# Lower parts of the first three weight blocks by TensorE and ScalarE, and the copy of an expert step's result moved behind the splits

## The chip, the cores and the metric

The kernel runs on one core of a Trainium2 chip. The metric is the device time of one execution in microseconds (us). A core has five engines that work beside each other, each through its own list of instructions in order: TensorE (PE in the profile; its weight loads are PEld), VectorE (DVE), ScalarE (ACT), GpSimd (POOL) and SyncE (SP), which here only starts transfers (DMA). An instruction that needs another engine's result waits for a semaphore, and everything behind it on its engine waits too.

## What is computed

Three layers in a row on 2 sequences of 768 tokens with 384 channels. First, a linear attention with 8 heads whose state decays by `w` per token. Second, a layer norm and a dense layer of width 1536 with a ReLU. Third, a mixture of 8 experts, where each token goes to one expert (or to that of the token before it, by a gate).

```python
def _attn_ref(r, k, v, w, u):
    for t in range(S):
        cur = np.einsum('bhd,bhe->bhde', u[None] * kt, vt)
        y[:, :, t] = np.einsum('bhd,bhde->bhe', rt, state + cur)
        state = w[None, :, :, None] * state + np.einsum('bhd,bhe->bhde', kt, vt)
def _moe_ref(x, g_ln, w_ch1, w_ch2):
    xn = (x - mu) / np.sqrt(var + 1e-06) * g_ln
    return x + np.maximum(xn @ w_ch1, 0.0) @ w_ch2
def _moe2_ref(x, w_gate, w_local, w1, w2):
    ...
            h = np.maximum(x[b, s] @ w1[e], 0.0)
            out[b, s] = p[e] * (h @ w2[e])
```

## The kernel before, in words

Products that need full precision are made of two numbers of the fast f32 form each: a high part (the value rounded by a copy into that type) and a low part (the value minus the high part). A product is then three fast matmuls: high by high, high by low, low by high.

**The first stretch, a list written out by hand.** Everything up to the experts is a list of small tasks in one string, `ORDER`; each word is a call (`w_lo:p.1` is the function `w_lo` on POOL for block 1), and each engine gets its instructions in the order of the words. The attention goes by pairs of (sequence b, group g of 128 tokens); the dense layer's weights come in 12 blocks f of 128 x 768. One block passes these tasks: `ld_c` (transfer of packed words), `dec0`, `dec1`, `dec2` on DVE (they unpack the words into one of two buffers, `d_[f % 2]`), `w_g` on ACT (three multiplications by the norm's gain), `w_hi` on ACT (high part into `wh`), `w_lo` on DVE or POOL (low part into `wl`). `dec0` of block f+2 overwrites the buffer that block f's last reader has used. Before the change `w_lo` runs on POOL for blocks 0 and 1 (`w_lo:p.0`, `w_lo:p.1`) and on DVE for block 2.

For a group of tokens the attention's tasks are: `kt`, `L`, `knt`, `rka`, `rkb` (products on DVE or POOL), `c` (sums; eight ACT instructions with their reads), `cv`, `at` (PE, 16 small matmuls), `am` (mask, DVE), `u` (PE), `us` (ACT copies it into the state `R`), `uw` (decay, by ACT, DVE or POOL), `ss`, `y` (PE), `yx` (DVE adds), `yq` (ACT squares), `yr`, `ym`, `ln` (norm, POOL or DVE), `lt` (PE turns the rows), `lh` and `ll` (high part on ACT, low part on DVE). Then the dense layer runs: `m1` (18 matmuls), `hh` (ACT), `hl` (DVE), `m2` per sequence. The first `m1` stands behind `lt.0.0` and `u.0.1` on PE.

**The experts.** For each expert e and each tile t of 128 of its tokens, `step(e, t)` is written out; steps with t > 0 stand in a branch that is taken when the expert has that many tokens. An engine that doesn't take the branch goes through a short piece of code that waits for its open transfers and then raises the semaphores by what the branch would have raised them. In this run the steps are (0,0), (1,0), (2,0), (2,1), (2,2), (3,0), (4,0), (4,1), (4,2), (5,0), (5,1), (6,0), (6,1), (7,0). The matmuls of a step: `first_pe` (first layer, banks 0 and 1; half of it for t = 0 at the step's head), `turn_pe` (turns the hidden layer of the step before), `xpose_pe` (turns gathered rows), `second` (second layer of the step before, into bank 4). On ACT and DVE: `xpose_split` and `turn_split` (high part on ACT, low part on DVE), `first_act` (ReLU), and for t = 0 `fl` (high and low parts of the coming weights). `result(o)` copies bank 4 into an output buffer on ACT and starts, on POOL, an indirect transfer that scatters it; `get` starts, on POOL, the indirect gather of a coming tile's rows into `x`, `xp` or `xe`. `rows(2,2)` is fetched by a `get` in step (2,0).

The order inside a step with t > 0 on ACT is: the copy of `result`, the high part of `xpose_split`, two high parts of `turn_split`, two `first_act`. For t = 0: the copy, one `fl`, two high parts of `turn_split`, `first_act`, two `fl`, `first_act`, `xpose_split`, three `fl`.

Of the kernel before, what the change touches and what calls it, by code (L numbers as in the profile page):

```python
# [49 lines left out]
y.1.0 w_g.2 ld_T.1.1 y.0.0 w_lo:p.1 ld_c.3 L:d.1.1.0 kt:p.1.1 yx.1.0 yq.1.0 ld_c.4 w_hi.2 cv:p.0.0.0 dec0.3 dec1.3 L:p.1.1.1  # L50
cv:p.0.0.1 yx.0.0 yq.0.0 yr.1.0 at.1.1 ym:d.1.0 ym:p.0.0 ln:p.1.0 lt.1.0 yr.0.0 ln:p.0.0 ld_k.0.1 knt:p.0.1 dec2.3 ld_v.0.1
w_lo:d.2 dec0.4 ss.0.0 dec1.4 dec2.4 w_g.3 w_hi.3 ld_v.1.1 lt.0.0 ld_k.1.1 lh.0.0 lh.1.0 w_g.4 w_hi.4 ll.0.0 w_lo:p.3 ld_T.0.1
ll.1.0 L:p.0.1.1 u.0.1 m1.0 ld_c.5 kt:p.0.1 L:p.0.1.0 dec0.5 dec1.5 dec2.5 w_g.5 w_lo:d.4 rka:d.1.1 sw:p.0.0 ld_c.6 dec0.6
rka:p.0.1 hh.0 rkb:p.0.1 dec1.6 w_hi.5 ld_c.7 hl.0 us.0.1 m1.1 hh.1 w_lo:p.5 dec2.6 hl.1 m2.0.0 m2.1.0 knt:p.1.1 dec0.7 dec1.7
m2.0.1 dec2.7 uw:p.0.1 ss.0.1 w_g.6 ld_c.8 w_hi.6 w_lo:p.6 am.1.1 ld_c.9 dec0.8 m2.1.1 dec1.8 c:a.0.1 rkb:p.1.1 w_g.7 at.0.1
am.0.1 w_hi.7 c:a.1.1 ld_c.10 m1.2 dec2.8 ld_k.1.2 w_g.8 hh.2 ld_k.0.2 w_lo:p.7 u.1.1 sw:p.1.0 m1.3 us.1.1 cv:p.1.1.0 cv:p.0.1.0
hh.3 w_hi.8 cv:p.1.1.1 dec0.9 dec1.9 hl.2 y.1.1 yx.1.1 dec2.9 yq.1.1 ym:a.1.1 y.0.1 cv:p.0.1.1 yx.0.1 yq.0.1 uw:p.1.1 consts
m2.1.2 hl.3 m2.0.2 w_g.9 w_hi.9 ym:d.0.1 m2.1.3 yr.1.1 ln:p.1.1 ss.1.1 lt.1.1 w_lo:d.8 yr.0.1 ln:d.0.1 dec0.10 ld_T.0.2 ld_c.11
lt.0.1 lh.0.1 m2.0.3 kt:p.0.2 w_lo:d.9 m1.5 sw:d.1.1 lh.1.1 ll.0.1 ll.1.1 m1.4 dec1.10 dec2.10 ld_T.1.2 kt:p.1.2 hh.5 L:p.1.2.1
hl.5 m2.1.5 m2.0.5 hh.4 dec0.11 w_g.10 w_hi.10 dec1.11 hl.4 m2.1.4 dec2.11 ld_v.0.2 w_g.11 rka:p.0.2 w_hi.11 rkb:p.0.2 m2.0.4  # L60
L:p.0.2.1 c:d.0.2 m1.7 hh.7 ld_v.1.2 rka:p.1.2 rkb:d.1.2 w_lo:d.11 w_lo:p.10 m1.6 sw:d.0.1 hl.7 hh.6 hl.6 c:d.1.2 m2.0.7
# [4 lines left out]
knt:d.1.3 yx.1.2 hh.11 rd.1.0 rl.0 hl.11 yr.0.2 knt:d.0.3 rm:d.0 m2.0.10 yq.1.2 yr.1.2 ln:p.0.2 rn.0 lt.0.2 rc.0 arg.0 ym:a.1.2
ln:p.1.2 lt.1.2 rkb:p.1.3 lh.0.2 lh.1.2 ll.0.2 m2.0.11 ll.1.2 ex.0 cv:p.0.3.0 L:p.0.3.1 x2.0.1 L:p.1.3.1 m2.1.11 x2.1.1 ld_v.0.4
row.0 m1.12 rr.0 hh.12 scan.0 col.0 L:d.1.3.0 oh.0 m1.13 hh.13 sum.0 hl.12 m2.1.12 rank.0 m1.14 pos.0 m2.0.12 c:d.1.3 hh.14
cv:p.0.3.1 hl.13 hl.14 m2.1.13 m2.0.13 ld_v.1.4 ld_k.1.4 m2.1.14 m2.0.14 sw:p.1.2 at.0.3 am.0.3 ld_T.0.4 cv:p.1.3.1 m1.15 hh.15
u.0.3 val.0 rw.0 tab.0 add.0 ld_k.0.4 m1.16 sw:a.0.2 us.0.3 hl.15 at.1.3 rka:p.0.4 m2.1.15 rt.0.1 uw:d.0.3 ss.0.3 y.0.3  # L70
rkb:p.0.4 c:a.0.4 ld_v.0.5 am.1.3 u.1.3 knt:p.1.4 yx.0.3 xs.0.1 us.1.3 uw:d.1.3 hh.16 yq.0.3 cv:p.0.4.1 re.0.1 ss.1.3 m1.17
xs.1.1 rt.1.1 y.1.3 hl.16 rd.0.1 re.1.1 ym:a.0.3 rd.1.1 m2.1.16 cv:p.1.3.0 yx.1.3 yq.1.3 hh.17 rka:d.0.5 hl.17 rl.1 m2.0.15
rm:a.1 rn.1 yr.0.3 sw:a.0.3 m2.0.16 ln:p.0.3 lt.0.3 rc.1 ym:p.1.3 arg.1 L:d.0.4.0 yr.1.3 ln:p.1.3 ld_T.1.4 L:p.1.4.1 lt.1.3
L:d.1.4.0 row.1 lh.0.3 lh.1.3 ll.0.3 rr.1 scan.1 ll.1.3 m2.1.17 x2.1.2 xs.1.2 m2.0.17 x2.0.2 rka:p.1.4 col.1 oh.1 m1.18 hh.18
# [4 lines left out]
uw:d.1.4 ss.1.4 y.1.4 hl.22 hl.23 L:p.0.5.0 yx.0.4 yq.0.4 arg.2 ex.2 yx.1.4 yr.0.4 ym:d.0.4 L:d.0.5.1 ln:d.0.4 yq.1.4 ym:a.1.4
m2.0.22 row.2 rr.2 scan.2 m2.0.23 xs.0.2 x2.0.3 m2.1.22 lt.0.4 yr.1.4 ln:d.1.4 lt.1.4 lh.0.4 rkb:d.1.5 sum.2 lh.1.4 sw:p.1.4  # L80
m2.1.23 cv:p.0.5.1 ld_T.1.5 rt.0.3 col.2 ll.0.4 at.0.5 knt:p.1.5 x2.1.3 ll.1.4 m1.24 L:p.1.5.0 am.0.5 hh.24 hl.24 oh.2 m1.25
knt:p.0.5 re.0.3 m2.1.24 xs.1.3 rt.1.3 xs.0.3 rank.2 m1.26 u.0.5 cv:d.0.5.0 rd.0.3 hh.25 hl.25 val.2 re.1.3 L:p.1.5.1 rd.1.3
# [1079 lines left out]
```

## Time and profile before

| | us |
|---|---|
| median of 3 runs | 461.54 (458.67 to 463.55) |
| the profiled execution | 460.63 |
| its span (first to last instruction) | 458.8 |
| PE busy | 390.6 (85%) |
| DVE busy | 310.3 (68%) |
| POOL busy | 203.9 (44%) |
| ACT busy | 187.7 (41%) |

Times in views count from the span's start. A row of the timeline has start, duration, engine, line, operation and `out<-in`; `[2.67 <-ACT xq L141]` says that the engine sat idle for 2.67 us before it and what ended that. `x3` is a run of three instructions merged into one row, whose duration reaches from the first to the last one's end. A busy engine isn't at its peak: matmuls overlap, so the step from one start to the next tells more of them than their durations. A name followed by q (ACTq, POOLq) is that engine's sequencer.

### The profile page before, as it was taken

To read this page: it belongs to the slowest core of one execution; us is meant where nothing else is said; L and a number is where in the kernel's file an instruction comes from. 1 tells how busy PE (TensorE), PEld (TensorE's weight loads), DVE (VectorE), ACT (ScalarE), POOL (GpSimd) and SP (SyncE) were. 2 spreads that over 40 slices of the span, in tenths; PEclk is the share of its full clock that TensorE was granted. 3 is DMA by queue.
4 is the path that set the end of the run, shared out by engine and by line. 5 is a ranking of instruction groups with operands and counts; after the bars stand their busy time and mean duration, and the time that the engine had idled before them with its cause. 6 is when DMAs were issued, how large, how long until landed. Compare 5 with 4: busy or idle time off the path is not lost. (4 is left out here: it accounts for less than half of the span.)

```text
span 458.8 us, 8752 instructions
## 1 busy us (share of the span) xinstructions
PE 390.6 (85%) x3297; PEld 356.0 (78%) x3297; DVE 310.3 (68%) x605; ACT 187.7 (41%) x447; POOL 203.9 (44%) x231
## 2 busy tenths in 40 slices
PE   1435496799979988999999999889889999999993
PEld 1434495799969978998999998777778788898883
DVE  7998999965873688478764877977711782265440
ACT  1365265331411441312131625448623872566450
POOL 5878978736361191128130020072453663423321
PEclk9999889899989999999999999999989999999997
...
GB/s 237 312 168 259 69 194 219 0 23 209 33 5 113 25 96 17 179 4 34 3 4 306 3 94 391 135 242 261 298 307 42 57 310 297 40 150 19 10 24 16
DMA packets 25360, 59.70 MB, mean 130 GB/s; under 512 B 4506, under 2 KB 11110, under 8 KB 25024
## 3 DMA queue, kind: packets, MB, share of 16 engines
...
HBM read 57.92 MB, written 5.70 MB: 139 GB/s over the span
## 5 line engine op out<-in xcount | busy, mean ns | idle before, releaser
L514 PE MATMUL banks<-wh,H 128*128 128x384 f32 x288 | 83.9, 353 | 8.1 <-DVE H L502 6.5
L981 PE MATMUL banks<-w1h,xq 128*128 128x512 f32 x168 | 59.3, 414 | 7.5 <-ACT xq L141 2.7
L514 PEld LDWEIGHTS banks<-wh,H 128*128 128x128 f32 x288 | 53.7, 193 | 10.3 <-DVE H L502 7.5
L146 DVE TENSOR_TENSOR w2l<-wb,w2h 128x1024 fp32r<-128x1024 f32 (+1 forms) x33 | 33.1, 1027 | 41.6 <-ACT w2h L141 41.3
L499 ACT ACTIVATE H<-banks 128x512 fp32r<-128x512 f32 x36 | 21.3, 594 | 78.5 <-PE banks L495 73.3
L514 PE MATMUL banks<-wl,H 128*128 128x384 f32 x144 | 49.3, 343 | 0.0
L1004 PE MATMUL banks<-w2h,H 128*128 128x384 f32 x224 | 46.4, 340 | 0.3 <-ACT H L141 0.3
L981 PEld LDWEIGHTS banks<-w1h,xq 128*128 128x128 f32 x168 | 32.2, 192 | 17.6 <-ACT xq L141 3.7
L495 PE MATMUL banks<-xq,wh 128*128 128x256 f32 x216 | 44.7, 305 | 0.4 <-DVE xq L478 0.4
L1004 PEld LDWEIGHTS banks<-w2h,H 128*128 128x128 f32 x224 | 39.2, 188 | 1.2 <-ACT H L141 0.5
L495 PEld LDWEIGHTS banks<-xq,wh 128*128 128x128 f32 x216 | 36.8, 207 | 1.1 <-DVE xq L478 0.6
L502 DVE SCALAR_TENSOR_TENSOR H<-banks,H 128x512 fp32r<-128x512 f32 x36 | 24.4, 684 | 17.7 <-ACT H L499 17.5
L202 POOL DMA_INDIRECT x<-xd,ids x17 | 20.0, 1179 | 34.4 <-issue 16.3
L981 PE MATMUL banks<-w1l,xq 128*128 128x512 f32 x84 | 34.1, 406 | 0.2 <-DVEq L1069 0.2
L146 DVE TENSOR_TENSOR w1l<-wa,w1h 128x512 fp32r<-128x512 f32 (+1 forms) x36 | 32.5, 952 | 0.4 <-ACT w1h L141 0.2
L495 PE MATMUL banks<-xq,wl 128*128 128x256 f32 x108 | 32.1, 297 | 0.0
L495 PE MATMUL banks<-xuh,wh 128*128 128x256 f32 x108 | 31.3, 290 | 0.0
L495 PE MATMUL banks<-xul,wh 128*128 128x256 f32 x108 | 30.6, 284 | 0.5 <-DVE xul L478 0.5
L495 PE MATMUL banks<-xuh,wl 128*128 128x256 f32 x108 | 30.5, 283 | 0.0
L141 ACT ACTIVATE w2h<-wb 128x1024 fp32r<-128x1024 f32 (+1 forms) x33 | 28.4, 900 | 3.1 <-DMA wb<-in_w 3.1
L372 POOL TENSOR_TENSOR cv<-R,c 64x384 f32<-64x384 f32 x19 | 18.7, 990 | 24.4 <-DVE c L367 22.7
L141 ACT ACTIVATE w1h<-wa 128x512 fp32r<-128x512 f32 (+1 forms) x36 | 28.1, 852 | 0.0
...
## 6 DMA issues: line engine op xcount, KB each, us to landing
...
```

What stands on the lines that cost most here:

```text
L141: ACT.activation(out=dst_hi, in_=src, func=ACTF.Relu if relu else ACTF.Copy)
L146: (lo_eng or DVE).tensor_tensor(out=dst_lo, in0=src, in1=dst_hi.bitcast(F32), op=ALU.subtract)
L202: POOL.indirect_dma_start(dst, None, xd[0:n, :], IndirectOffsetOnAxis(ap=off, axis=0), bounds_check=n - 1, oob_is_err=False)
L372: e.tensor_tensor(out=r3(cv[b][s], NH), in0=r3(R[b][g % 2][s, q, :], NH), in1=bc(c[s], [64, NH, HD]), op=ALU.mult)
L495: PE.matmul(out=ph[:, i, :], lhsT=a, rhs=x_[:, k, :], start=(q == 0), stop=(q == 8))
L499: ACT.activation(out=hh[:, ring(n)], in_=r3(B[3 + n % 2], 2), func=ACTF.Relu)
L502: DVE.scalar_tensor_tensor(out=hl[:, ring(n)], in0=r3(B[3 + n % 2], 2), scalar=0.0, in1=hh[:, ring(n)].bitcast(F32), op0=ALU.max, op1=ALU. ...
L514: PE.matmul(out=bank_o(b, g), lhsT=a[:, f2, s][:, i], rhs=w_[:, 2 * p + i, DM:], start=(p + i + n == 0), stop=(p == NP - 1 and i == 1 and ...
L981: PE.matmul(out=B[n], lhsT=a_[:, k, t], rhs=w_[:, k, n * 512:n * 512 + 512], start=(last == 0 and q == 0), stop=(last == 1 and q == KD - 1))
L1004: PE.matmul(out=B[4][:, 0:DM], lhsT=a_[:, k, 0:128], rhs=w_[:, k, :], start=(q == 0), stop=(q == 23))
```

## The change

Two parts. First, the lower parts of blocks 0, 1 and 2 are made by PE and ACT: `lo_pe` puts ident x block minus ident x high part into banks 3 and 4 (for each half a matmul of plain f32 and one of the fast form with the negated identity, which `negid` writes once into an unused corner of `H`), and `lo_act` copies both banks into `wl`. `w_lo` of these three blocks leaves POOL and DVE. Second, `result(o)` in `step` moves from behind `turn_pe` to behind `turn_split`.

```diff
 ORDER = """
...
+rka:d.1.0 at.0.0 rkb:p.1.0 w_g.0 w_hi.0 wlp.0 am.1.0 u.1.0 dec0.1 dec1.1 dec2.1 c:a.1.0 wla.0 w_g.1 cv:d.1.0.1 ld_k.0.0
+knt:p.0.0 w_hi.1 wlp.1 us.1.0 am.0.0 ld_v.0.0 u.0.0 rka:p.0.0 rkb:d.0.0 c:a.0.0 us.0.0 uw:a.0.0 wla.1 cv:p.1.0.0 ld_c.2 dec0.2
...
+        neg = H[:, 1, KE - 1, 0:128]
+
+        def negid():
+            ACT.activation(out=neg, in_=ident, func=ACTF.Copy, scale=-1.0)
+
+        def lo_pe(f):
+            for i in range(2):
+                c = slice(i * DM, i * DM + DM)
+                PE.matmul(out=B[3 + i][:, 0:DM], lhsT=ident, rhs=d_[f % 2][:, c].bitcast(F32), start=True, stop=False)
+                PE.matmul(out=B[3 + i][:, 0:DM], lhsT=neg, rhs=wh[:, f, c], start=False, stop=True)
+
+        def lo_act(f):
+            ACT.activation(out=wl[:, f].rearrange("p (i d) -> p i d", i=2), in_=BB[:, 3:5, 0:DM], func=ACTF.Copy)
...
             if before is not None:
                 for n in range(2):
                     turn_pe(n)
-                result(o)
             if t:
                 xpose_split(1)
                 first_pe(e, 1, 0, 1)
...
             if before is not None:
                 for n in range(2):
                     turn_split(n)
+                result(o)
             first_act(e, t, 0)
```

In the list, `wlp` is `lo_pe` and `wla` is `lo_act`. The order of DVE, POOL and SP changes only by the three `w_lo` that go. On PE, between the second group's first products and the next attention product, before the change (d_116 and d_117 are the two block buffers, R, L and knt those of the attention, 111 and 131 of sequence 1, 109 and 130 of sequence 0):

```order
L405 MATMUL banks<-R_111,knt_131 48x48 x16
L405 MATMUL banks<-R_109,knt_130 48x48 x16
L441 MATMUL banks<-R_111,L_125 64x48 x16
L441 MATMUL banks<-R_109,L_124 64x48 x16
L388 MATMUL banks<-L_125,kt_123 64x64 x16
```

The same place on PE after the change, from the second half of `lo_pe` of block 1 on (lines are 15 higher in the changed file):

```order
L309 MATMUL banks<-d_117,cs 128x384
L310 MATMUL banks<-wh,H 128x384
L420 MATMUL banks<-R_109,knt_130 48x48 x16
L456 MATMUL banks<-R_111,L_125 64x48 x16
L456 MATMUL banks<-R_109,L_124 64x48 x16
L309 MATMUL banks<-d_116,cs 128x384
L310 MATMUL banks<-wh,H 128x384
L309 MATMUL banks<-d_116,cs 128x384
L310 MATMUL banks<-wh,H 128x384
L403 MATMUL banks<-L_125,kt_123 64x64 x16
```

`lo_pe` of block 1 now stands ahead of `u.0.0`, and that of block 2 ahead of `at.1.1`, behind which `lt.1.0` and `lt.0.0` follow.

On ACT, from `us.0.0` on, before the change:

```order
L412 ACTIVATE R_109<-banks 48x384
L421 ACTIVATE ws_134<-R_109,wC 48x48 x8
L292 ACTIVATE d_116<-d_116,gt_s 128x128 x3
L456 ACTIVATE xh_75,sq_143<-x_72,sx_139 128x384
L295 ACTIVATE wh<-d_116 128x768
L456 ACTIVATE xh_74,sq_142<-x_72,sx_138 128x384
```

The same place on ACT after the change:

```order
L427 ACTIVATE R_109<-banks 48x384
L436 ACTIVATE ws_134<-R_109,wC 48x48 x8
L313 ACTIVATE wl<-banks 128x768
L292 ACTIVATE d_116<-d_116,gt_s 128x128 x3
L471 ACTIVATE xh_75,sq_143<-x_72,sx_139 128x384
L295 ACTIVATE wh<-d_116 128x768
L471 ACTIVATE xh_74,sq_142<-x_72,sx_138 128x384
L313 ACTIVATE wl<-banks 128x768
```

`lo_act` of block 1 stands between `uw:a.0.0` and `w_g.2`, ahead of `yq.1.0`; that of block 2 behind `yq.0.0`.

On ACT in the experts, step (2,0) and the head of step (2,1), before the change (x_147, xh_74 are output buffers, w1h and w2h high parts of weights, H the turned hidden layer):

```order
L1010 ACTIVATE xh_74<-banks 128x384
L141 ACTIVATE w2h_2944<-wb_2535 128x1024
L141 ACTIVATE H<-banks 128x4x128 x2
L986 ACTIVATE hs<-banks,tab 128x512
L141 ACTIVATE w2h_2944<-wb_2535 128x1024 x2
L986 ACTIVATE hs<-banks,tab 128x512
L141 ACTIVATE xq<-banks 128x3x128
L141 ACTIVATE w1h_2536<-wa_2946 128x1024 x3
L762 TENSOR_LOAD nt_i
L1069 COMPARE_AND_BRANCH
L1010 ACTIVATE x_147<-banks 128x384
L141 ACTIVATE xq<-banks 128x3x128
```

The same place after the change, from the splits of the turned layer on:

```order
L141 ACTIVATE H<-banks 128x4x128 x2
L1025 ACTIVATE xh_74<-banks 128x384
L1001 ACTIVATE hs<-banks,tab 128x512
L141 ACTIVATE w2h_2957<-wb_2548 128x1024 x2
L1001 ACTIVATE hs<-banks,tab 128x512
L141 ACTIVATE xq<-banks 128x3x128
L141 ACTIVATE w1h_2549<-wa_2959 128x1024 x3
L777 TENSOR_LOAD nt_i
L1084 COMPARE_AND_BRANCH
L141 ACTIVATE xq<-banks 128x3x128
L141 ACTIVATE H<-banks 128x4x128 x2
L1025 ACTIVATE x_147<-banks 128x384
```

The copy (L1010, now L1025) stands behind the two splits into H, in a step with t = 0 as in one with t > 0; `xq` of a step with t > 0 is now its first ACT instruction.

## Rows read from the trace of the kernel before

**Rows 1.** Busy time by stretch: us, PE, PEld, DVE, ACT, POOL, PEclk, DMA.

```profile
20.00:45.00 25.00, 11.44 (x168) 9.82 (x169) 22.79 (x28) 13.92 (x48) 20.20 (x18) 1.00 0.65 219
...
110.00:330.00 220.00, 205.56 (x1990) 189.79 (x1989) 160.37 (x424) 81.83 (x203) 71.10 (x84) 0.99 0.33 117
```

**Rows 2.** Waits of PE over the whole span: us in total, times, longest.

```profile
PE banks L514 <- DVE H L502: 6.5, 2, 5.0
...
PE banks L981 <- ACTq L1069: 2.3, 3, 0.9
...
PE banks L208 <- DMA x<-xd,ids: 1.2, 1, 1.2
```

**Rows 3.** Timeline of the first 64 us, single rows of four engines.

```profile
10.42 1.97 PE L388 MATMUL banks<-L,kt 48*64 48x64 f32 x32
...
17.43 1.81 POOL L298 TENSOR_TENSOR wl<-d,wh 128x768 fp32r<-128x768 f32 x1
...
17.75 1.90 DVE L277 TENSOR_SCALAR d<-wq 128x768 int32<-128x768 int32 x1
...
20.56 1.52 PE L405 MATMUL banks<-R,knt 64*48 64x48 f32 x32 [1.62 <-POOL knt L353]
...
24.04 0.84 ACT L295 ACTIVATE wh<-d 128x768 fp32r<-128x768 f32 x1
...
29.04 0.46 ACT L412 ACTIVATE R<-banks 48x384 f32<-48x384 f32 x1
...
29.54 1.91 ACT L421 ACTIVATE ws<-R,wC 48x48 f32<-48x48 f32 x8
...
31.46 0.99 ACT L292 ACTIVATE d<-d,gt_s 128x128 f32<-128x128 f32 x3
...
34.54 0.56 DVE L277 TENSOR_SCALAR d<-wq 128x768 int32<-128x768 int32 x1
...
34.65 0.61 ACT L456 ACTIVATE xh<-x,sx 128x384 f32<-128x384 f32 x1 [2.20 <-DVE x L445]
...
41.48 0.90 PE L469 MATMUL banks<-cs,xh 128*128 128x128 f32 x3 [1.62 <-POOL xh L464]
...
42.94 1.02 DVE L478 TENSOR_TENSOR xq<-banks,xq 128x384 fp32r<-128x384 f32 x2 [0.71 <-ACT xq L473]
...
44.89 1.68 DVE L277 TENSOR_SCALAR d<-wq 128x768 int32<-128x768 int32 x1 [0.93 <-POOL wl L298]
...
60.39 0.52 PE L514 MATMUL banks<-wl,H 128*128 128x384 f32 x1
...
60.71 0.84 PE L514 MATMUL banks<-wh,H 128*128 128x384 f32 x2
```

**Rows 4.** Timeline of steps (2,1) and (2,2), single rows of three engines.

```profile
330.65 0.49 PE L208 MATMUL banks<-cs,x 128*128 128x128 f32 x3
...
333.76 0.49 ACT L1010 ACTIVATE x<-banks 128x384 f32<-128x384 f32 x1 [3.75 <-DMA out<-first_o,oi]
...
334.69 0.79 PE L981 MATMUL banks<-w1h,xq 128*128 128x512 f32 x1 [2.67 <-ACT xq L141]
...
335.85 1.00 POOL L202 DMA_INDIRECT x<-xd,ids  x1 [0.31 <-ACT H L141]
...
344.66 0.49 PE L208 MATMUL banks<-cs,x 128*128 128x128 f32 x3
...
345.79 0.50 PE L981 MATMUL banks<-w1h,xq 128*128 128x512 f32 x1
```

**Rows 5.** Busy time by stretch about that gap, columns as in rows 1.

```profile
332.00:334.60 2.60, 0.01 (x1) 0.00 (x0) 0.00 (x0) 0.84 (x3) 0.11 (x1) 1.00 0.59 198
334.60:338.00 3.40, 3.31 (x8) 2.64 (x9) 1.78 (x3) 1.01 (x3) 2.79 (x3) 0.50 0.88 276
```

**Rows 6.** Instructions of the branch's line on POOL, 326 to 335 us.

```profile
L1069 POOLq INC_SWDGE_SEM  x1: 485/485/485, 333.1 to 333.1; - x1
```

**Rows 7.** Gathers that POOL issued between 335.5 and 337 us.

```profile
DMA to landing us min/median/max: 7.9/8.0/8.1
```

More of the change, by code (lines that the diff above doesn't have):

```diff
@@ L50 @@
[L50 to L61, printed above, removed]
@@ L66 @@
[L66 to L74, printed above, removed]
@@ L79 @@
[L79 to L82, printed above, removed]
@@ L91 @@
-lw.1 x2.1.5 rt.0.5 re.0.5 ext.0 exh.0 rd.0.5 rt.1.5 xs.1.5 exl.0 re.1.5 rd.1.5 ext.1 exh.1 exl.1 rl.5 rm:d.5 e1.1 f0.2 f0.10
-zX.0 rn.5 rc.5 arg.5 e1.0 row.5 f0.7 f0.1 f0.9 f0.8 f0.11 ex.5 sum.5 e1.2 e1h.1 e1l.1 rr.5 scan.5 col.5 e1h.0 e1l.0 oh.5 val.5
-rank.5 pos.5 e1h.2 e1l.2 e1.3 e1h.3 e2.0.0 rw.5 e1l.3 pk finn tab.5 e2.0.1 add.5 fini f0.6 e2o.0 f0.4 f0.0 f0.3 xs.0.5 get.0.0
-get.1.0 get.0.1 f0.5 f1.2 e2.1.0 cnt0 e2.1.1 e2o.1 xt0.0 xh0.0 xl0.0 zX.1 f1.5 f1.0 lw.2 f1.1
-f1.3 e2s.0 f1.4
+wkt wkn negid at.1.0 ld_T.0.0 L:p.0.0.1 ld_v.1.0 ld_un dec0.0 L:p.0.0.0 dec1.0 dec2.0 ld_k.1.0 knt:p.1.0 kt:d.0.0 ld_c.1
@@ new lines @@
+rka:d.1.0 at.0.0 rkb:p.1.0 w_g.0 w_hi.0 wlp.0 am.1.0 u.1.0 dec0.1 dec1.1 dec2.1 c:a.1.0 wla.0 w_g.1 cv:d.1.0.1 ld_k.0.0
+knt:p.0.0 w_hi.1 wlp.1 us.1.0 am.0.0 ld_v.0.0 u.0.0 rka:p.0.0 rkb:d.0.0 c:a.0.0 us.0.0 uw:a.0.0 wla.1 cv:p.1.0.0 ld_c.2 dec0.2
+dec1.2 dec2.2 uw:d.1.0 ss.1.0 y.1.0 w_g.2 ld_T.1.1 y.0.0 ld_c.3 L:d.1.1.0 kt:p.1.1 yx.1.0 yq.1.0 ld_c.4 w_hi.2 wlp.2 cv:p.0.0.0
+dec0.3 dec1.3 L:p.1.1.1 cv:p.0.0.1 yx.0.0 yq.0.0 wla.2 yr.1.0 at.1.1 ym:d.1.0 ym:p.0.0 ln:p.1.0 lt.1.0 yr.0.0 ln:p.0.0 ld_k.0.1
@@ new lines @@
+knt:p.0.1 dec2.3 ld_v.0.1 dec0.4 ss.0.0 dec1.4 dec2.4 w_g.3 w_hi.3 ld_v.1.1 lt.0.0 ld_k.1.1 lh.0.0 lh.1.0 w_g.4 w_hi.4 ll.0.0
+w_lo:p.3 ld_T.0.1 ll.1.0 L:p.0.1.1 u.0.1 m1.0 ld_c.5 kt:p.0.1 L:p.0.1.0 dec0.5 dec1.5 dec2.5 w_g.5 w_lo:d.4 rka:d.1.1 sw:p.0.0
+ld_c.6 dec0.6 rka:p.0.1 hh.0 rkb:p.0.1 dec1.6 w_hi.5 ld_c.7 hl.0 us.0.1 m1.1 hh.1 w_lo:p.5 dec2.6 hl.1 m2.0.0 m2.1.0 knt:p.1.1
+dec0.7 dec1.7 m2.0.1 dec2.7 uw:p.0.1 ss.0.1 w_g.6 ld_c.8 w_hi.6 w_lo:p.6 am.1.1 ld_c.9 dec0.8 m2.1.1 dec1.8 c:a.0.1 rkb:p.1.1
@@ new lines @@
+w_g.7 at.0.1 am.0.1 w_hi.7 c:a.1.1 ld_c.10 m1.2 dec2.8 ld_k.1.2 w_g.8 hh.2 ld_k.0.2 w_lo:p.7 u.1.1 sw:p.1.0 m1.3 us.1.1
+cv:p.1.1.0 cv:p.0.1.0 hh.3 w_hi.8 cv:p.1.1.1 dec0.9 dec1.9 hl.2 y.1.1 yx.1.1 dec2.9 yq.1.1 ym:a.1.1 y.0.1 cv:p.0.1.1 yx.0.1
+yq.0.1 uw:p.1.1 consts m2.1.2 hl.3 m2.0.2 w_g.9 w_hi.9 ym:d.0.1 m2.1.3 yr.1.1 ln:p.1.1 ss.1.1 lt.1.1 w_lo:d.8 yr.0.1 ln:d.0.1
+dec0.10 ld_T.0.2 ld_c.11 lt.0.1 lh.0.1 m2.0.3 kt:p.0.2 w_lo:d.9 m1.5 sw:d.1.1 lh.1.1 ll.0.1 ll.1.1 m1.4 dec1.10 dec2.10
+ld_T.1.2 kt:p.1.2 hh.5 L:p.1.2.1 hl.5 m2.1.5 m2.0.5 hh.4 dec0.11 w_g.10 w_hi.10 dec1.11 hl.4 m2.1.4 dec2.11 ld_v.0.2 w_g.11
@@ L811, in moe_kernel @@
         tasks = dict(ld_wt=ld_wt, zR=zero_R, zeros=zeros, powers=powers, table=table, decay=decay, wkc=wkc, wkt=wkt, wkn=wkn, consts=consts, ld_cs=ld_cs, ld_un=ld_un, ld_gt=ld_gt,
-                     ld_T=ld_T, ld_k=ld_k, ld_v=ld_v, ld_c=ld_c, dec0=dec0, dec1=dec1, dec2=dec2, w_g=w_g, w_hi=w_hi, w_lo=w_lo,
+                     ld_T=ld_T, ld_k=ld_k, ld_v=ld_v, ld_c=ld_c, dec0=dec0, dec1=dec1, dec2=dec2, w_g=w_g, w_hi=w_hi, w_lo=w_lo, negid=negid, wlp=lo_pe, wla=lo_act,
                      kt=a_kt, L=a_L, knt=a_knt, rka=a_rka, rkb=a_rkb, c=a_c, cv=a_cv, at=at_pe, am=at_m, u=u_pe, us=u_s, uw=u_w, ss=s_s, sw=s_w,
```

54 lines of the change are left out of this document (35 added, 19 removed).

## The prediction

> **What bounds the kernel now.** I read the busy time by stretch first: in 20 to 45 us PE is busy for 11.44 of 25 us and DVE for 22.79, in 110 to 330 us PE for 205.56 of 220 [rows 1]. So the kernel has an opening in which DVE, POOL and ACT prepare what PE lacks, and then a long part bound by PE. A microsecond won in the opening moves all that follows; in the long part only PE's own waits count. Second, PE's waits: the longest of the opening behind the first products is 5.0 us for DVE (the lower half of H); in the experts they are short, three of 2.3 us together for ACT's sequencer and one of 1.2 us for a gather [rows 2], but for one: at 334.69 us PE had waited 2.67 us for ACT's xq, and xq stood behind the copy of a result that had itself waited 3.75 us [rows 4]. These two places are what the change touches, so I read the timeline there.
>
> **Part 1, lower parts of blocks 0 to 2.** What goes: two subtractions on POOL (1.81 us the one in the rows) and one on DVE. They cost more than their own time: dec0 takes 1.90 us on DVE beside the POOL subtraction and 0.56 us where POOL is idle [rows 3]. So DVE gets back roughly its own subtraction and 1.3 us twice. That is a gain only if DVE is what the next thing waits for, and the trace says where it is tested: dec0 of block 5 at 44.89 us waited 0.93 us, not for DVE's own work but for POOL's lower part of block 3 [rows 3]. POOL gets there through yr, ln, knt in an unbroken row that starts when ACT's yq.1.0 is done (34.65 us). So the question is when yq.1.0 starts.
>
> What comes: per block four matmuls on PE and a copy of 128 x 768 on ACT, and once a 128 x 128 copy, which falls into idle time of ACT before the first block. The fast matmuls of 384 columns step by 0.32 us at the pace PE has there (60.39 to 60.71) [rows 3]. A plain f32 matmul of 384 columns isn't in the trace. The nearest are those of L388: 16 in the program, 32 in the trace, so each is two records; 32 take 1.97 us, 0.123 us for one of 64 columns, or 0.74 us scaled to 384. Lower end: two records at the fast pace, 0.64 us. Upper end: the pair of an L388 step goes from opposite halves of the partitions to opposite halves of the outputs, so two may run beside each other, and one alone takes 0.246, or 1.47 us scaled. I take 1.3, near the upper end, because the code of L388 does address separate quarters. A block then costs 2 x 1.3 + 2 x 0.32 = 3.2 us (1.9 to 3.6).
>
> The Trainium skill, "FP8 and Floating Point Precision", section "TensorE Precision Notes", says that true FP32 takes four passes through the array. By that a matmul would be an estimated 4 x 0.32 = 1.28 us and the sum below would stay as it is; by the row without overlap (0.74) the opening would win 1.9 us instead of 0.85. No run here shows the passes themselves, only the two records.
>
> Now the chain. DVE's dec2 of block 1 stays where it was, since POOL is busy without a break until then with or without its subtraction. w_hi.1 ends at 24.04 + 0.84 = 24.9 us. PE then does lo_pe.1 (to 28.1) and only then u.0.0 (1.52, to 29.6), which before ran at 20.56. ACT: us.0.0 0.46 (to 30.1), uw.0.0 1.91 (32.0), lo_act.1, priced as w_hi of the same shape, 0.84 (32.8), w_g.2 0.99 (33.8), and yq.1.0 starts at 33.8 instead of 34.65 [rows 3]: 0.85 us won, because ACT had waited 2.20 us for DVE there and this slack is now filled. The second arm: yq.1.0 0.7, w_hi.2 0.84 (35.4), lo_pe.2 on PE (38.6), at.1.1 of L388's form 1.97 (40.6), two turnings of 0.90 (42.4), lh and ll with 1.0 us of DVE: 44.0, as before (42.94 + 1.02) [rows 3], and just in time for a dec0.5 at 44.0. So the opening wins 0.85 us. At 1.9 us per block it is 34.65 - 32.5 = 2.1; at 3.6 the second arm ends at 44.8 and nothing is left. From 45 to 95 us DVE has next to no idle time, and then PE; nothing there takes the 0.85 back.
>
> **Part 2, the copy behind the splits.** In a step with t > 0, xq no longer stands behind the copy. Elsewhere bank 4 is ready when the copy comes, and the copy is hidden by PE's turning; the place that counts is (2,1). There the copy waited until POOL, which ran behind, had left the branch of expert 1 (it raised its semaphores at 333.1 us) [rows 6]. Now xq goes as soon as xpose_pe is done. In step (2,2) first_pe starts 1.13 us after the step's L208; so (2,1)'s would start at 330.65 + 1.13 = 331.8 instead of 334.69, 2.9 us sooner [rows 4]. And the granted clock, 0.50 (1.2 GHz) from 334.6 to 338.0 after that gap and 1.00 before [rows 5], wouldn't fall there, which gives back half of 3.4 us, 1.7.
>
> But what is late next is close by: PE would be at the head of (2,2) at 344.66 - 2.9 - 1.7 = 340.05, and its rows come by the gather that POOL issued at 335.85, with 7.9 to 8.1 us to landing [rows 4, 7]: 343.85. POOL issues it there because it waits in the same branch for the same transfer, which this change doesn't touch. Before, the rows had landed 0.8 us ahead of PE; now PE waits 3.8 us for them and is 0.8 us ahead of before. A gap of 2.67 us was enough for the clock to fall to 0.50 [rows 4, 5]; the new one is longer, so I charge the same 1.7 us again, behind it. Net at (2,2): -0.8 + 1.7 = +0.9.
>
> Steps with t = 0: the copy (0.49 us) moves from in front of one fl, where ACT soon waits for PE anyway, to the middle of a chain without idle time that ends with fl and the branch. Where the next step is also t = 0, PE waits for that end (2.3 us in three places) [rows 2]. The first of them, into (1,0), has no copy ahead of it. Into (2,0) the 0.49 us is swallowed by the 1.2 us for which PE then waits for a gather [rows 2]; into (4,0) it isn't: +0.5. Where a step with t > 0 follows, the copy is saved there and paid here: nothing. POOL's scatter waits 3 to 4 us more for its copy in a few steps, and POOL's queue (the next gathers) with it; POOL idles longer than that before the gathers that follow, and the last scatter of the program isn't moved.
>
> **Sum.** The profiled execution took 460.63 us, 1.8 more than its span; -0.85 - 0.8 + 1.7 + 0.5 = +0.55: 461.2 us. The median of the runs shown (461.54) is 0.9 above the profiled one, inside their spread of 5 us, and I leave that out. About 1% is what a measurement of this kernel can tell from no change.
>
> **The rivals.** *The gain in the experts stays.* If the gather lands 3 to 4 us sooner, PE keeps the 2.9 + 1.7 us: 460.63 - 0.85 - 4.6 + 0.5 = 455.7. For it: 8.0 us is long, with the DMA engines busy 0.88 of the time there [rows 5], and another run may have them freer. Against: the weights' transfers that fill them are issued at the same point. 16%.
>
> *TensorE's line makes the opening slower.* lo_pe.1 and lo_pe.2 both stand ahead of what the first m1 needs, so every us that a block costs above 3.7 comes twice, by u.0.0 and by at.1.1 and the turnings. If the weight loads of plain f32 aren't hidden (about another 0.33 us for each of four records), a block costs 4.9 us: w_hi.2 at 37.1, lo_pe.2 to 42.0, turnings to 45.8, ll to 48, dec0.5 some 2.4 us later than before. With part 2: 460.63 + 2.4 + 1.4 = 464.4. For it: PE is in order and at low pace there. Against: more matmuls may raise the clock before block 2, and weight loads are hidden elsewhere. 12%.
>
> *The step isn't freed at all.* If xq in (2,1) still can't go before 333.8 for another reason, only the opening and (4,0) are left: 460.63 - 0.85 + 0.5 = 460.3. Against: after the move it waits for PE alone. 12%.
>
> **How the numbers follow.** My own case has 60%, with 459.0 (block cost 1.9 us, a clock that partly holds) to 463.0 (no gain in the opening, both losses, a gather 1 us later). The range for 8 in 10 takes in most of the first rival and of the second: 456.0 to 464.5. Faster by over 1% (below 456.9) is most of the first rival, 0.13; slower by over 1% (above 466.2) a tail of the second and of unseen costs, 0.07; within 1%, 0.80.
>
> **What would show it.** Right: yq.1.0 starts about 0.8 us sooner and dec0.5 near 44.0; no wait for xq at (2,1), and instead PE waiting 3 us or more at L208 (now in its line of the changed file) for a gather, with a clock of 0.50 behind it; PE's wait into (4,0) near 1.0. Wrong: a wait for rows at (2,2) below 1 us (first rival), ll or dec0.5 later than before (second), xq still late at (2,1) (third), or a granted clock of 1.00 behind the wait at (2,2), which takes 1.7 us off the forecast.

## The result, and the profile after

The changed kernel took 454.04 us (median of 4 runs, 451.83 to 455.50), the kernel before 462.27 (4 runs, 458.67 to 463.55). The ratio on record is 0.9888, 95% interval 0.9842 to 0.9934: 1.1% faster, where no change was forecast (461.2 us, range 456.0 to 464.5). It is not the quotient of these two medians, which is 0.982; in the later comparisons the kernel before came to 457.05 (29 runs), 457.45 (22) and 456.75 us (11). A second measurement of the changed kernel gave 0.9866 (0.9826 to 0.9907). The profiled execution took 453.58 us with a span of 451.8, 7.0 less than before; PE is busy for 396.6 us (390.6 before), DVE for 302.2 (310.3), POOL for 205.9, ACT for 190.2.

Busy time by stretch, the changed kernel, columns as in [rows 1]:

```profile
20.00:45.00 25.00, 20.43 (x248) 15.54 (x247) 22.12 (x28) 15.94 (x51) 20.65 (x18) 0.80 0.66 223
105.00:321.00 216.00, 204.72 (x1976) 188.59 (x1975) 155.04 (x423) 78.80 (x201) 71.75 (x84) 0.98 0.33 114
```

In the opening PE is busy for 20.43 us instead of 11.44, with the new matmuls. The clock column, 0.80 for 1.00, is no sign of a slower pace than before; the last section says why. DVE is nearly as full as before. PE's waits over the span, beside [rows 2]:

```profile
PE banks L529 <- DVE H L517: 6.5, 2, 5.0
PE banks L208 <- DMA x<-xd,ids: 4.3, 2, 3.0
...
PE banks L996 <- ACTq L1084: 2.7, 3, 0.9
```

The 5.0 us for DVE's half of H are still there, the wait for xq at (2,1) is gone from the list, the waits for gathers grew from 1.2 to 4.3 us, and those into the next expert from 2.3 to 2.7. So the list of waits doesn't show where the gain came from; the place in time of that 5.0-us wait does. Timeline of the opening, the changed kernel, single rows of four engines (compare [rows 3]):

```profile
17.63 0.56 DVE L277 TENSOR_SCALAR d<-wq 128x768 int32<-128x768 int32 x1
...
17.77 1.27 POOL L368 TENSOR_TENSOR knt<-kn,Wkn 128x384 f32<-128x384 f32 x1 [0.40 <-DMA kn<-in_kn]
...
17.87 1.65 PE L309 MATMUL banks<-d,cs 128*128 128x384 f32 x2
...
21.37 0.93 PE L420 MATMUL banks<-R,knt 64*48 64x48 f32 x32
...
23.21 0.91 PE L309 MATMUL banks<-d,cs 128*128 128x384 f32 x2 [0.91 <-ACT d L292]
...
24.10 0.56 DVE L374 TENSOR_TENSOR rn<-rn,kn 128x384 f32<-128x384 f32 x1
24.58 0.55 DVE L277 TENSOR_SCALAR d<-wq 128x768 int32<-128x768 int32 x1
...
24.70 0.24 ACT L380 ACTIVATE rn<-rn 128x48 f32<-128x48 f32 x1 [0.29 <-DVE rn L374]
...
25.27 0.92 PE L420 MATMUL banks<-R,knt 64*48 64x48 f32 x32
...
26.16 0.96 DVE L285 SCALAR_TENSOR_TENSOR d<-wq,d 128x768 int32<-128x768 int32 x1
...
26.52 0.47 ACT L427 ACTIVATE R<-banks 48x384 f32<-48x384 f32 x1
...
30.52 0.61 ACT L471 ACTIVATE xh<-x,sx 128x384 f32<-128x384 f32 x1
...
40.22 1.67 DVE L277 TENSOR_SCALAR d<-wq 128x768 int32<-128x768 int32 x1 [0.93 <-POOL wl L298]
...
53.01 1.01 PE L529 MATMUL banks<-wh,H 128*128 128x384 f32 x2 [5.00 <-DVE H L517]
```

The same instructions in the kernel before, those that [rows 3] doesn't have:

```profile
21.35 1.64 DVE L285 SCALAR_TENSOR_TENSOR d<-wq,d 128x768 int32<-128x768 int32 x1
...
24.96 1.82 POOL L298 TENSOR_TENSOR wl<-d,wh 128x768 fp32r<-128x768 f32 x1 [1.29 <-ACT wh L295]
...
25.56 1.63 DVE L359 TENSOR_TENSOR rn<-rn,kn 128x384 f32<-128x384 f32 x1
27.11 1.61 DVE L277 TENSOR_SCALAR d<-wq 128x768 int32<-128x768 int32 x1
...
27.22 0.24 ACT L365 ACTIVATE rn<-rn 128x48 f32<-128x48 f32 x1 [1.97 <-DVE rn L359]
...
29.75 1.47 DVE L285 SCALAR_TENSOR_TENSOR d<-wq,d 128x768 int32<-128x768 int32 x1
...
57.66 1.01 PE L514 MATMUL banks<-wh,H 128*128 128x384 f32 x2 [5.01 <-DVE H L502]
```

DVE runs the same list without a break in both, but four of its operations are shorter: dec0 of block 1 0.56 for 1.90, the product rn 0.56 for 1.63, dec0 of block 2 0.55 for 1.61, dec2 of block 2 0.96 for 1.47. That is 1.34 + 1.07 + 1.06 + 0.51 = 3.98 us; with a start 0.12 sooner, dec2 of block 2 ends at 27.12 instead of 31.22. yq.1.0 (ACT L471) starts at 30.52 instead of 34.65, dec0 of block 5 at 40.22 instead of 44.89, and the product that waits for DVE's half of H, the anchor of what follows here, at 53.01 instead of 57.66: 4.65 us.

How much of this repeats is seen in the other traces, whose kernels come below. The last three of the four operations are as short in all eight traces without the two subtractions on POOL, and 1.46 to 1.64, 1.61 or 1.62, and 1.47 us in the five with them: 2.5 to 2.7 us together. The first is not as steady: dec0 of block 1 took 0.56 to 1.12 us without and 0.88 to 1.92 with them. The anchor stands at 53.01 to 54.55 in the four traces with the changed opening (after, after_again, lower_only, gate_after) and at 56.80 to 57.73 in the four with the opening of before (before, copy_only, matmuls_only, gate_before). So 3.6 us, the difference of the means, is a better size for the opening's gain than 4.65.

The span lost 7.0 us: 4.65 up to the anchor, 1.95 from there to the first product of the experts (296.50 for 303.10), 0.4 in the experts. The 1.95 are mostly two gains and a loss. Routing of group 0, timeline of the kernel before (L594 to L602 are DVE's short operations, L613 the two matmuls that turn their flags):

```profile
128.51 0.86 DVE L597 TENSOR_TENSOR eq<-eq,cs 128x16 f32<-128x16 f32 x1
129.29 1.30 DVE L599 TENSOR_TENSOR f__163<-f__163,cs 128x2 f32<-128x2 f32 x1
130.63 1.20 DVE L600 TENSOR_SCALAR fg<-f__163 128x2 bf16<-128x2 f32 x1
...
128.51 0.82 POOL L372 TENSOR_TENSOR cv<-R,c 64x384 f32<-64x384 f32 x1
...
131.88 0.22 PE L613 MATMUL banks<-cb,fg 128*2 128x128 bf16 x1 [1.62 <-DVE fg L600]
132.77 0.22 PE L613 MATMUL banks<-cb,fg 128*2 128x128 bf16 x1 [0.67 <-DVE fg L602]
```

and of the changed kernel:

```profile
123.95 0.16 DVE L612 TENSOR_TENSOR eq<-eq,cs 128x16 f32<-128x16 f32 x1
124.04 0.79 DVE L614 TENSOR_TENSOR f__163<-f__163,cs 128x2 f32<-128x2 f32 x1
124.86 1.22 DVE L615 TENSOR_SCALAR fg<-f__163 128x2 bf16<-128x2 f32 x1
...
123.95 0.86 POOL L387 TENSOR_TENSOR cv<-R,c 64x384 f32<-64x384 f32 x1
...
126.13 0.22 PE L628 MATMUL banks<-cb,fg 128*2 128x128 bf16 x1 [0.42 <-DVE fg L615]
127.34 0.22 PE L628 MATMUL banks<-cb,fg 128*2 128x128 bf16 x1 [0.99 <-DVE fg L617]
```

An operation on 16 values takes 0.16 us, or as long as the POOL operation beside it: the one that starts in the same hundredth as POOL's cv took 0.86 us in one trace and 0.16 in the other. PE waits 2.29 or 1.41 us for the flags, and in the first case its granted clock then falls to 0.50. Group 1 shows longer waits too, without a fall of the clock: 1.35 and 0.84 us for 0.60 and 0.51, and 1.64 for 0.61 us for DVE's er right behind. By the table below the two groups are 2.14 and 2.15 us, together 4.29 us of the profiled difference. And 2.3 us go the other way in front of the experts: behind a wait of PE for DVE's er the clock fell to 0.50 in the changed kernel (1.94 us), and stayed at 1.00 in the one before (1.95 us). The change touches nothing there; the clock fell at this place in seven of the thirteen traces, copy_only among them.

Steps (2,1) and (2,2) of the changed kernel, timeline of two engines, beside [rows 4]:

```profile
325.03 0.49 ACT L141 ACTIVATE xq<-banks 128x384 fp32r<-128x384 f32 x1 [1.05 <-PE banks L208]
...
327.27 0.49 ACT L1025 ACTIVATE x<-banks 128x384 f32<-128x384 f32 x1 [0.67 <-DMA out<-xh,top_i]
...
337.28 0.55 PE L208 MATMUL banks<-cs,x 128*128 128x128 f32 x3 [3.02 <-DMA x<-xd,ids]
```

and its busy time about the last of these, beside [rows 5]:

```profile
334.20:337.20 3.00, 0.05 (x1) 0.00 (x0) 0.00 (x0) 0.00 (x0) 1.26 (x2) 1.00 0.87 318
337.20:341.00 3.80, 3.72 (x22) 3.27 (x23) 1.83 (x3) 1.91 (x4) 1.22 (x2) 1.00 0.07 23
```

xq stands ahead of the copy and waits for PE alone, PE then waits 3.02 us for gathered rows, and behind that wait the granted clock is 1.00.

### The profile page after: what moved, and what is told of

The parts are those of the page before. It is cut to its first block, busy times and chain, and to the rows that moved or that the text cites. A ratio compares the mean times of both kernels' runs of the same rounds, so it can differ in the third digit from the quotient of the medians.

```text
span 451.8 us, 8787 instructions
## 1 busy us (share of the span) xinstructions
PE 396.6 (88%) x3315; PEld 358.3 (79%) x3315; DVE 302.2 (67%) x604; ACT 190.2 (42%) x451; POOL 205.9 (46%) x229
## 5 line engine op out<-in xcount | busy, mean ns | idle before, releaser
L529 PE MATMUL banks<-wh,H 128*128 128x384 f32 x288 | 85.2, 357 | 8.6 <-DVE H L517 6.5
L529 PEld LDWEIGHTS banks<-wh,H 128*128 128x128 f32 x288 | 54.8, 196 | 10.9 <-DVE H L517 7.5
L996 PE MATMUL banks<-w1h,xq 128*128 128x512 f32 x168 | 58.3, 408 | 5.1 <-ACTq L1084 2.7
L510 PE MATMUL banks<-xq,wh 128*128 128x256 f32 x216 | 42.0, 293 | 0.4 <-DVE xq L493 0.4
L510 PEld LDWEIGHTS banks<-xq,wh 128*128 128x128 f32 x216 | 34.5, 194 | 1.1 <-DVE xq L493 0.6
L146 DVE TENSOR_TENSOR H<-banks,H 128x512 fp32r<-128x512 f32 x28 | 18.0, 686 | 22.9 <-ACT H L141 22.9
L510 PE MATMUL banks<-xq,wl 128*128 128x256 f32 x108 | 30.8, 285 | 0.0
```

The source lines that it names most:

```text
L146: (lo_eng or DVE).tensor_tensor(out=dst_lo, in0=src, in1=dst_hi.bitcast(F32), op=ALU.subtract)
L510: PE.matmul(out=ph[:, i, :], lhsT=a, rhs=x_[:, k, :], start=(q == 0), stop=(q == 8))
L529: PE.matmul(out=bank_o(b, g), lhsT=a[:, f2, s][:, i], rhs=w_[:, 2 * p + i, DM:], start=(p + i + n == 0), stop=(p == NP - 1 and i == 1 and ...
L996: PE.matmul(out=B[n], lhsT=a_[:, k, t], rhs=w_[:, k, n * 512:n * 512 + 512], start=(last == 0 and q == 0), stop=(last == 1 and q == KD - 1))
```

## The experiments

Two theories stood at the start. *Relief*: without the subtractions on POOL, DVE's operations in the opening are shorter, and that alone moves the anchor. *Pace*: the added matmuls keep PE at its upper clock level, and PE hands the attention's products over sooner. Rivals: the moved copy carries the gain; the long part's 1.95 us belong to the change. Expectations on record call the anchor "the first product of the second weights"; the one meant is the first that waits for DVE's half of H.

**lower_only.** The changed kernel, the copy back at its place.

```diff
                 for n in range(2):
                     turn_pe(n)
+                result(o)
...
                     turn_split(n)
-                result(o)
```

> The changed kernel with the result copied at its old place, so only the lower parts of blocks 0 to 2 change. Theory (the gain is the opening's: VectorE no longer meets GpSimd's subtractions there): the first product of the second weights at 53.0 us instead of 57.7, and a time 4 to 5 us under the kernel before, a ratio near 0.990. Rival (the moved copy carries the gain): opening as much earlier, but given back by the experts, ratio 0.998 or above.

Measured 453.79 us, ratio 0.9901 (0.9862 to 0.9940); anchor at 53.87, where 53.0 was expected. The lower parts alone give the gain.

**copy_only.** The kernel before with the same move the other way.

> The kernel before with the copy of the result moved behind the splits and nothing else. Theory: the opening stands as before (first product of the second weights at 57.7 us), the wait of ScalarE's split into step (2,1) goes, the wait for the gathered rows at (2,2) eats most of it, and the time is 0 to 1 us under before: ratio 0.998 to 1.000. Rival (the copy carries the gain): ratio 0.993 or below.

Measured 456.58 us, ratio 0.9987 (0.9956 to 1.0017). The copy carries no gain that the time shows. The anchor came at 56.80, 0.86 sooner than in before, with the same opening: so far two executions differ by themselves.

**matmuls_only.** The kernel before, `negid` and `lo_pe` added at their three places, the sums read by nobody.

```diff
-... w_g.0 w_hi.0 w_lo:p.0 am.1.0 ...
+... w_g.0 w_hi.0 w_lo:p.0 wlp.0 am.1.0 ...
```

> The kernel before with the added products of TensorE at their places, their sums read by nobody; the lower parts are still subtracted on GpSimd and VectorE. Relief theory: VectorE's operations stay as long as before (1.9 us for the masking of block 1), the first product of the second weights at 57.5 us or later, ratio 1.000 to 1.006. Pace theory: TensorE's clock rises near 21 us as in the changed kernel and the first product of the second weights comes at 55 us or earlier, ratio 0.996 or below.

Measured 456.26 us, ratio 0.9982 (0.9954 to 1.0009), a little below the 1.000 to 1.006 expected. Timeline of two engines:

```profile
17.75 1.92 DVE L278 TENSOR_SCALAR d<-wq 128x768 int32<-128x768 int32 x1
...
19.96 0.92 PE L417 MATMUL banks<-R,knt 64*48 64x48 f32 x32
...
57.73 1.01 PE L526 MATMUL banks<-wh,H 128*128 128x384 f32 x2 [5.01 <-DVE H L514]
```

PE's products are quicker (0.92 us for the 1.52 of [rows 3]), DVE is as slow as before, and the anchor stays (57.73). Pace alone gives no gain that shows.

**no_lower.** The kernel before without these lower parts; POOL fills their tile with a constant.

```diff
-w_lo:p.0   w_lo:p.1   w_lo:d.2
+POOL.memset(wl[:, 0:3].bitcast(F32), 2.0 ** -14)
```

> The kernel before without the lower parts of blocks 0 to 2: neither GpSimd and VectorE nor TensorE and ScalarE work them out; GpSimd fills their tile with a constant once, in the first 7 us. Two theories on the opening's 4.65 us. Relief of VectorE and GpSimd: VectorE's last decoding step of block 2 ends near 27 us as in the changed kernel (31.2 before), and the first product of the second weights stands at 53 us or earlier, ratio 0.990 or below. TensorE's pace: without the added products TensorE stays at its lower clock to 30 us as before, and the first product of the second weights stays at 56 us or later, ratio 0.996 or above.

Measured 454.22 us, ratio 0.9934 (0.9912 to 0.9957), anchor at 56.15: between the two. The filling spoiled it: DVE's table stood behind it, an operation on 128 x 8 took 2.77 us, and dec0 of block 0 ended 3.9 us late. Inconclusive, so once more with ACT filling the tile.

**no_lower2.**

```diff
+for f in range(3):
+    ACT.activation(out=wl[:, f], in_=bc(wt_s[:, 0:1], [128, 2 * DM]), func=ACTF.Copy, scale=2.0 ** -14)
```

> The kernel before without the lower parts of blocks 0 to 2, as no_lower, but the constant in their tile is written by ScalarE in its idle time before 10 us, so that VectorE starts as early as before. Relief theory: masking of block 1 starts at 17.1 to 17.8 us and takes at most 1.1 us (1.9 before), VectorE's last decoding step of block 2 ends at 26.5 to 28 us (31.2 before), the product that waits for VectorE's half of H stands at 52.5 to 54 us (57.7 before), ratio 0.987 to 0.991. Pace theory: that product at 56 us or later, because TensorE stays at its low clock, ratio 0.996 or above.

Measured 452.77 us, ratio 0.9893 (0.9833 to 0.9953); the anchor:

```profile
53.63 1.01 PE L514 MATMUL banks<-wh,H 128*128 128x384 f32 x2 [5.02 <-DVE H L502]
```

Without the work anywhere, the anchor stands 0.24 us ahead of lower_only's 53.87 and among the 53.01 to 54.55 of the four kernels with the work on PE and ACT. So relief explains the opening, and PE and ACT do the moved work at no cost that shows. (dec2 of block 2 ended at 28.2, just behind the 28 expected.)

**blocks01** and **block2.** lower_only with `w_lo:d.2` kept on DVE, and with `w_lo:p.0` and `w_lo:p.1` kept on POOL.

> Copy at its old place, lower parts of blocks 0 and 1 by TensorE and ScalarE, block 2 on VectorE as before. If the relief of GpSimd carries the gain: the product that waits for VectorE's half of H at 53.5 to 55 us (57.7 before, 53.9 with all three blocks), ratio 0.990 to 0.994. If VectorE's own subtraction of block 2 carries it: at 56.5 us or later, ratio 0.997 or above.

> Copy at its old place, lower part of block 2 alone by TensorE and ScalarE, blocks 0 and 1 on GpSimd as before. If the relief of GpSimd carries the gain: VectorE as before up to 34 us, the product that waits for VectorE's half of H at 56.7 to 58.5 us, ratio 0.997 to 1.003. If VectorE's own subtraction of block 2 carries it: at 55 us or earlier, ratio 0.993 or below.

Measured 456.41 us, 0.9933 (0.9882 to 0.9983), anchor at 54.36; and 457.52 us, 0.9983 (0.9946 to 1.0020), anchor at 57.03. Against 57.66 the two POOL subtractions give 3.30 us and DVE's own one 0.63; their sum, 3.93, is near lower_only's 3.79. As anchors of one opening differ by 0.9 us and more, 0.63 is better read from a shorter stretch: from yq.1.0 to dec0 of block 5 it is 10.23 to 10.28 us in the five traces with block 2's subtraction on DVE and 9.70 in block2, 0.5 us less. From dec0 of block 5 to the anchor it is 12.77 to 12.80 us in every trace but early_half.

**after_again.** The changed kernel once more.

> The changed kernel as it is, once more: what stays the same from one execution to the next, and what doesn't. Theory (opening and copy are fixed gains, the middle is a matter of where GpSimd's and VectorE's operations fall): the product that waits for VectorE's half of H within 1 us of 53.0, TensorE's clock at 1.00 behind the wait for the gathered rows at (2,2), while the stretch from that product to the first product of the experts (243.5 us in the first trace) differs by up to 4 us; ratio 0.986 to 0.992. Rival (the profiled execution shows fixed times throughout): that stretch within 0.5 us of 243.5.

Measured 451.19 us, ratio 0.9866. Its profiled execution was a long one (456.31 us): anchor at 54.55, 1.5 us behind the first trace where under 1 was expected; the stretch to the experts 244.58 us (243.49 in the first trace), so the two traces of one kernel differ there by 1.1, more than the rival's 0.5 and less than the 4 that I allowed for; clock 1.00 behind the wait at (2,2).

The long part came apart when all traces stood side by side. Worked out from the timelines: the anchor; ACT's 12th to 13th high part of H (L499 before), a stretch with the routing of group 0; its 18th to 19th, with that of group 1; first matmul of the second layer in step (2,0) to that in (4,0).

```
                anchor   group 0   group 1   (2,0) to (4,0)
before          57.66     14.45     13.12        44.7
after           53.01     12.31     10.97        43.9
after_again     54.55     13.82     10.97        43.9
lower_only      53.87     13.18     10.97        44.1
copy_only       56.80     12.31     10.98        43.3
matmuls_only    57.73     12.31     10.98        44.3
no_lower        56.15     12.30     10.98        43.8
no_lower2       53.63     14.04     10.98        44.3
blocks01        54.36     12.30     10.98        44.0
block2          57.03     12.30     10.98        44.3
gate_before     57.55      9.95      8.92        44.4
gate_after      53.87      9.97      8.92        43.5
early_half      50.59      9.97      8.92        45.5
```

The profiled execution of before is the worst of the ten without gates in both routing columns, and kernels with nothing of the change stand at 12.31 and 10.98 like the changed one. So these 4.29 us of the profiled difference aren't the change's.

**gate_after** and **gate_before.** If DVE's short operations are stretched by POOL's long ones, POOL can be held back until they are done: one small copy that reads the last flags, in the routing of groups 0 and 1, ahead of POOL's next long operation.

```diff
-lt.1.2 rkb:p.1.3 ...          ln:p.1.3 ld_T.1.4 L:p.1.4.1
+lt.1.2 gate.0 rkb:p.1.3 ...   ln:p.1.3 gate.1 ld_T.1.4 L:p.1.4.1
+        def rt_gate(g):
+            POOL.tensor_copy(out=fgs, in_=fg[:, 1, :])
```

> The changed kernel with one more small copy on GpSimd in each of the first two routing stages: it reads the flags that VectorE writes last, so GpSimd's big operations behind it start only when VectorE's short operations are done. Theory (VectorE's short operations of routing are stretched from 0.16 to as much as 1.3 us by GpSimd's big ones, and TensorE waits for their flags): no operation of that group over 0.6 us, TensorE's waits for the flags (1.4 and 1.1 us in the changed kernel) under 0.3 us, 1.5 to 4 us less than the changed kernel, ratio to before 0.980 to 0.986. Rival (GpSimd's later start makes other work late): waits go but the ratio is 0.988 or above.

> The kernel before with the two small copies on GpSimd in the routing stages, as gate_after, and nothing of the change. If the routing stages are lost time of their own, apart from the opening: TensorE's waits for the flags (2.3 and 2.2 us before) under 0.3 us, the opening as before (57 to 58 us), ratio 0.986 to 0.992. If the gate pays only together with the change: ratio 0.996 or above.

gate_after: 447.28 us, ratio 0.9781 (0.9724 to 0.9837), below the 0.980 to 0.986 expected. gate_before: 450.61 us, 0.9872 (0.9831 to 0.9913). Routing of group 0, timeline of gate_after, three engines (last row: group 1):

```profile
123.88 0.16 DVE L613 TENSOR_TENSOR dl<-lg,m__152 128x16 f32<-128x16 f32 x1
...
124.27 0.17 DVE L617 TENSOR_SCALAR fg<-f__164 128x2 bf16<-128x2 f32 x1
...
124.77 0.19 POOL L622 COPY fgs<-fg 128x2 bf16<-128x2 bf16 x1 [0.91 <-DVE fg L619]
124.92 1.02 POOL L376 TENSOR_TENSOR rn<-rn,kn 128x384 f32<-128x384 f32 x1
...
126.52 0.22 PE L633 MATMUL banks<-cb,fg 128*2 128x128 bf16 x2
...
160.60 0.22 PE L633 MATMUL banks<-cb,fg 128*2 128x128 bf16 x2
```

The short operations are at 0.16 us, PE waits for no flag, and POOL's wait of 0.91 us delays nothing that the two stretches show. The two stretches shrink by 2.36 and 2.06 us against the usual 12.31 and 10.98. The product of the ratios for the change and for the gates, 0.9888 x 0.9872 = 0.976, is within the interval for both together: two separate gains.

**early_half.** gate_after, and DVE's first two halves of H ahead of the decoding of block 6. With it ACT's `us.0.1` comes behind `hh.1`.

```diff
-dec0.6 rka:p.0.1 hh.0 rkb:p.0.1 dec1.6 w_hi.5 ld_c.7 hl.0 us.0.1 m1.1 hh.1 w_lo:p.5 dec2.6 hl.1 m2.0.0
+rka:p.0.1 hh.0 rkb:p.0.1 hl.0 w_hi.5 m1.1 hh.1 hl.1 dec0.6 dec1.6 ld_c.7 us.0.1 w_lo:p.5 dec2.6 m2.0.0
```

> The kernel with the gates, and VectorE's first two halves of H put ahead of the decoding of block 6 in its order. If the order on VectorE alone holds the product up: it comes at 50 to 50.5 us (53.9 with the gates), the 5.0-us wait falls to about 1.5, and the time is 2 to 4 us under gate_after, ratio to before 0.970 to 0.975. If VectorE's whole load of decoding sets the end of the opening: the product comes as early, but the next waits for VectorE grow by as much, ratio 0.976 to 0.980.

Measured 446.66 us, ratio 0.9768 (0.9731 to 0.9804): no different from gate_after. Timeline of PE:

```profile
50.59 1.01 PE L531 MATMUL banks<-wh,H 128*128 128x384 f32 x2 [1.27 <-DVE H L519]
...
63.77 0.39 PE L512 MATMUL banks<-xq,wl 128*128 128x256 f32 x1 [1.73 <-POOL wl L300]
...
328.82 0.55 PE L209 MATMUL banks<-cs,x 128*128 128x128 f32 x3 [2.44 <-DMA x<-xd,ids]
```

and the busy time about the last wait:

```profile
326.00:328.80 2.80, 0.39 (x3) 0.06 (x1) 0.00 (x0) 0.00 (x0) 1.25 (x2) 1.00 1.01 370
328.80:333.00 4.20, 4.18 (x19) 3.51 (x20) 1.83 (x3) 1.91 (x4) 1.24 (x2) 0.67 0.37 143
```

The anchor comes 3.28 us sooner, close to what was expected of the order. By the routing of group 0, 2.7 of that are gone to later waits (its flags at 125.92 for 126.52); 1.4 come back in front of the experts, where the clock had fallen in gate_after and here does not (the first product of the experts at 289.41 for 291.42); and at (2,2) the 2.0 that are left go too: PE waits 2.44 us for rows (1.60 in gate_after), and this time the clock falls behind it. gate_after and early_half are both faster than the kernel before, and by their medians than the changed one.

## Why the prediction was right only at its edge

The change was worth more than forecast, and the range holds it by luck. 454.04 us lies below the 456.0 to 464.5; by the ratio, on the 461.54 us of the kernel before, it is 456.4, just inside. The lower end had been put there for a rival that did not come about. The order of events was right; the size failed at two terms of the sum.

*The opening, -0.85, measured -4.65 in the two first traces and -3.6 on the mean of four and four.* The step that failed is "PE then does lo_pe.1 (to 28.1) and only then u.0.0 (1.52, to 29.6)", with ACT's us.0.0 straight behind it. In the changed kernel PE's first matmul of block 1 went at 23.21, before w_hi.1 had ended (24.03), block 1 took 2.06 us for the 3.2 of the sum and u.0.0 0.92 for 1.52, so PE was done at 26.19. What us.0.0 (26.52 for the 29.6 of the sum) then waited for was ACT's eight instructions of `c.0.0` in front of it, a row that the sum doesn't have, and these start when DVE's product rn is done: 24.66 instead of 27.19. Of the six traces with block 1 moved to PE, c.0.0 ended last in four (after, lower_only, early_half, blocks01); in gate_after the two ended together, at 27.5, and in after_again u.0.0 did, at 28.45, both with a granted clock of 0.50 in that stretch. From us.0.0 to yq.1.0 it is 4.00 us, where the sum has 4.2, and from there the chain is the one forecast: POOL's row to the lower part of block 3, then dec0 of block 5, which still waits 0.93 us for it.

So DVE's relief, which the prediction prices at "roughly its own subtraction and 1.3 us twice", had no place in its chain. The sentence that kept it out, "DVE's dec2 of block 1 stays where it was, since POOL is busy without a break until then", matters less: dec2 of block 1 ended at 21.53 instead of 22.99 here, but at 23.00 in after_again, whose anchor is 3.1 us sooner all the same. What moved in every trace lies behind it: from the end of dec2 of block 1 to that of block 2 it is 8.23 to 8.25 us in the five traces with the subtractions on POOL and 5.07 to 6.81 in the eight without. I had read dec0's 1.90 and 0.56 us in [rows 3] rightly as the price of meeting POOL, and then asked only whether POOL is busy. But what DVE pays depends on which of its operations meets which of POOL's: with the 1.81-us subtractions gone POOL waited for a transfer at 17.4 us, dec0 of block 1 slipped in ahead of it, and POOL, ahead of its order, sat idle for 2.93 us up to 26.69, beside rn and dec0 and dec1 of block 2. The Trainium skill, "SBUF — State Buffer", section "SBUF: two separate sides", says that POOL and a DVE operation that runs in a two-port mode or has two inputs in SBUF take a shared port pair for a whole operation, and that the loser fully blocks. The traces agree: dec0 of block 1 began 0.32 us after POOL's subtraction and ended 0.41 us behind that one's end [rows 3].

*The block's cost on PE and ACT, 3.2 us (1.9 to 3.6).* Block 0 takes from 17.87 to 21.37, 3.5 us; block 1, which is the one in the chain, took 2.06 at the faster pace, near the lower end. It did not show in the time: no_lower2 does without it and its anchor is 0.24 us ahead of lower_only's. The Trainium skill's four passes ("FP8 and Floating Point Precision", "TensorE Precision Notes") made an estimated 1.28 us a matmul; block 0 gives (3.5 - 2 x 0.32) / 2 = 1.43.

*The copy, -0.8 + 1.7 + 0.5, measured -0.6.* No wait for xq at (2,1); the arrival at (2,2) 0.78 us sooner against the first product of the experts (337.28 - 296.50 for 344.66 - 303.10), as summed; PE's waits for gathers up by 3.0 us there; 0.38 us more into (4,0). What failed is the second 1.7 us, "I charge the same 1.7 us again, behind it": the clock stayed at 1.00, the counter-case that the forecast named. From (2,0) to (4,0) the eight traces with the copy at its old place average 44.25 us, four of the five with it moved 43.6, and early_half, where the clock fell, 45.5. So the move is worth 0.6 us, or costs 1.2; the time can't show it (copy_only, 0.9987).

*The rivals.* None came about as told. The gain in the experts didn't stay, since the gather was late as summed; TensorE's line didn't hold the opening up (in its own sum, 4 x 0.33 on 3.2 gives 4.5 us a block, and 4.9 only on the upper end of 3.6; its ll comes out at 47.4 rather than 48); (2,1) was freed. The chance of 0.13 for faster by over 1% stood on the first of them; 1.1% came for a reason that I hadn't listed, DVE's relief.

*The reference.* I set the sum against one execution of 460.63 us. Its routing had cost 2.1 us more than usual in each of two groups, and in front of the experts it had been spared 2.3.
